# Turning a block of outputs back behind the next block's products in four steps of a fused attention and Fourier-mixing kernel, with four smaller changes of order and buffers

## The chip, the core and the metric

The kernel runs on one core of one Trainium2 chip. The metric is the device time of one execution in microseconds (us); lower is better. Three runs of the kernel before took 765.33, 768.76 and 773.62 us, so its median is 768.76 us. One execution was profiled; it took 765.44 us.

## What is computed

The first half is a decayed linear attention over 4 batches, 8 heads, 768 positions and 64 columns, in blocks of 64 positions with a running state:

```python
intra = np.einsum('bhic,bhjc->bhij', qb, kb) * Dmask[None]
intra = np.einsum('bhij,bhjd->bhid', intra, vb)
inter = np.einsum('bhid,bhde->bhie', qb * lam_pow[None], kv_state)
out[:, :, sl] = intra + inter
kv_state = lam_block[None, :, None, None] * kv_state + np.einsum('bhsd,bhse->bhde', kb_dec, vb)
```

Its output, laid out as x of shape 4 x 768 x 512, goes through a Fourier mix, a normalization and a two-layer network:

```python
mixed = np.real(np.fft.fft(np.fft.fft(x, axis=1), axis=2))
u = x + mixed
un = (u - mu) / np.sqrt(var + 1e-06)
ch = np.maximum(un @ w_ch1, 0.0) @ w_ch2
return u + ch
```

The weights come in as 64-bit floats and are converted on the chip to 32-bit ones.

## The kernel before, in words

The work lies in three stages.

**Attention** (the generator `attention`) goes through 12 steps, three per batch (SC = 3), each of 256 positions in two chunks of 128. Step i begins where the previous one has left scores in SBUF and the state's share of the output in PSUM, and then issues, in this order: `turn_k(i + 1)` and `turn_q(i + 1)`, which transpose the next keys and queries on TensorE and copy them to SBUF (L400, L401, L406, L407); `back(i - 1)`, which transposes the previous step's outputs `oT` back to rows (L476) and copies them out twice, once mirrored (L483 to L487, for one chunk L500 and L501); `to_state(i + 1)`, the products that add to the running state (L415) and VectorE's or ScalarE's reads of them (L425, L423); `within(i)`, the products of scores and values (L456) and the copies of the outputs to `oT` (L461); the loads of the values two steps on and the keys and queries three steps on; and `begin(i + 1)`: the next scores (L435), their reads with the decay mask (L441), GpSimd's scaling of the keys (L395) and decay of the state (L430), and the state's share of the next outputs (L450). `turn_q` also makes the queries times the powers of the decay, `qs`, on VectorE (L409); before, it reads the same PSUM tile as ScalarE's copy L407.

Each engine's order in this stage is the order in which the code is written (`strict`), interleaved by hand with the rest: after each of the three yields of a step, `PLAN` names units of other work. "w" is a third of a 512-column piece of weight conversion (L266, L267, L268, then L271, then L274 and L275: ScalarE does L267, VectorE the rest), "m" a unit of the Fourier mix of batch 0, "l" and "k" units of the first network layer. `REST` is the string of units behind the attention.

PSUM has eight banks, held by number here: pa_96 to pa_99 are banks 0 to 3 and go round for `psum_t` (transposes and scores); pa_100 and pm_101 are banks 4 and 5, the outputs being summed (`psum_o`); pm_102 and pm_103 are banks 6 and 7 and go round for `psum_a` and `psum_m`. Behind the attention `rest` is set so that all eight go round.

`oT` has one buffer: its copies (L461) wait until the previous outputs have been transposed (L476).

**Mix and first groups.** Then a scheduler orders the Fourier mix of batches 1 to 3, the normalization and the network for the first four groups of 256 rows (L735, L945, L952, L954, L960), beside the rest of the weight conversion. The first groups transpose their normalized rows in `turned_u` (L870, L871).

**Eight later groups in pairs.** The rest of the network runs as four pairs of groups with a seven-product scheme in two levels (L1230 for the first layer of pair 0, L1323 and L1397 otherwise, with VectorE's sums of the products, L1332 and L1405). `load_u(1)` loads the second pair's input into `ur` (L1093, two loads of 512 KB each). `ur` has one buffer, and the first pair's second layer uses it from SBUF as scratch for `sums_of_first`, four pieces at a time, written to memory through GpSimd's queue (L320, L322). Products' right-hand sums come from memory as `tx` (L1104, 256 KB each). L1140 is VectorE's first use of `ur`.

Of the kernel before, what the change touches and what calls it, by code (L numbers as in the profile page):

```python
# [17 lines left out]
ALU = mybir.AluOpType  # L18
# [59 lines left out]
def kernel(  # L78
# [69 lines left out]
    def P(i):  # L148
        return keep(i) if strict[0] else i
# [253 lines left out]
    def turn_q(i):  # L403
        for ch in range(2):
            pt = psum_t([128, HP, C])
            lead(P(nc.tensor.transpose(pt[:, hp, :], q_of[i % 2][:, ch, 128 * hp:128 * hp + 128], ident)) for hp in range(HP))  # L406
            P(nc.scalar.copy(qT[:, :, C * ch:C * ch + C], pt))  # L407
            if i % SC + ch:
                P(nc.vector.tensor_tensor(qs[:, :, C * ch:C * ch + C], pt, qpow, op=ALU.mult))  # L409

    def to_state(i):
        n, vt, kd = i % SC, v_of[i % 2], k_of[i % 2]
        chunks = (0, 1) if n < SC - 1 else (0,)
        pu = [(psum_t if unread[0] or i < 2 else psum_a)([128, HP, D]) for _ in chunks]
        lead(P(mm(pu[ch][HD[hi], hp, :], lhsT=kd[HD[ch], 2 * hp + hi, r, :], rhs=vt[HD[ch], 2 * hp + hi, r, :],  # L415
                start=(hp + r == 0), stop=(r == 1), skip_group_check=True))
             for hp in range(HP) for r in range(2) for ch in chunks for hi in range(2))
        with tc.high_priority(100):
            for ch in chunks:
                c = 2 * n + ch  # L420
                s_new = states[(c + 1) % 3]
                if c == 0:
                    P(nc.scalar.copy(s_new, pu[ch]))  # L423
                else:
                    P(nc.vector.tensor_tensor(s_new, s_new, pu[ch], op=ALU.add))  # L425
                if c < NC - 2 and ch == 0:
                    decayed(c + 1)
# [43 lines left out]
        if n == SC - 1:  # L471
            P(nc.vector.tensor_copy(z[:, :, 0:1], first))

    def turned(o, cols):
        px = psum_t([C, HP, 128])
        lead(P(nc.tensor.transpose(px[:, hp, :], o[:, hp, cols], ident)) for hp in range(HP))  # L476
        return px.rearrange("p h e -> p (h e)")

# [7 lines left out]
        P(nc.scalar.copy(x[0:n, 0:HM], px[0:n, 0:HM]))  # L486
        P(nc.scalar.copy(x[0:n, HM:DM], px[0:n, DM - 1:HM - 1:-1]))  # L487

    def back(i):
        b, n = divmod(i, SC)  # L490
        for ch in range(2):
            c = 2 * n + ch
            last = c == NC - 1
            cols = slice(C * ch, C * ch + C)
            if b in TURNED:
                if not last:
                    x = xn_[b, c] = new(xp, [C, DM], "x")
                    px = turned(oT[i], cols)
                    if n == 1 and ch == 0:
                        P(nc.vector.tensor_copy(x[:, 0:HM], px[:, 0:HM]))  # L500
                        P(nc.vector.tensor_copy(x[:, HM:DM], px[:, DM - 1:HM - 1:-1]))  # L501
                    else:
                        put(px, x)
                continue
            inside = b == INSIDE
            x = new(xn, [C, DM], "xn") if inside and c >= HC else new(xp, [C, DM], "x")
            if inside:
                xn_[b, c] = x
            put(turned(oT[i], cols), x, crossed=bool(ch))
            if c == 0:  # L510
                xd[b] = (dram.tile([S - 256, DM], F32, name=f"xa{b}"), dram.tile([257, DM], F32, name=f"xb{b}"),
                         dram.tile([C, DM], F32, name=f"xc{b}"))
                P(nc.sync.dma_start(xd[b][1][256:257], x[0:1]))
                if not inside:
                    P(nc.sync.dma_start(xd[b][2], x))
            elif not last:
                P(nc.sync.dma_start(xd[b][0][(c - 1) * C:c * C], x))
            if c >= NC - 2:
                P(nc.sync.dma_start(xd[b][1][(c - NC + 2) * C:(c - NC + 3) * C], x))
        if b not in TURNED or n == 0:  # L520
            return
        if n == 1:
            eo[b] = new_eo()
        work = [(2 * n - 1, oTs[i - 1]), (2 * n, oTs[i])]
        if n == SC - 1:
            work.append((2 * n + 1, oTs[i]))
        for m, o in work:
            px = turned(o, slice(C, 2 * C) if m % 2 == 0 else slice(0, C))
            if m < HC:
                put(px, eo[b][HC - 1 - m][1][:, 1, 0:DM][0:BLK[HC - 1 - m]], BLK[HC - 1 - m])  # L530
            else:
                u = xs[b, HC + NC - 1 - m] = new(xp, [128, DM], "x")
                put(px, u)
        if n == SC - 1:
            for t in range(HC):
                xs[b, t] = xn_.pop((b, t))

    def attention():

        n = B * SC  # L540

        def begin(i):
            first_ = from_state if i == n - 1 else scores
            first_(i)
            if i == 0:
                to_state(i)
            if i + 1 < n and i != n - 1:
                P(nc.gpsimd.tensor_copy(scored, sc[0][:, 0, 0, 0:1]))
                scale(i + 1)
            (scores if i == n - 1 else from_state)(i)  # L550
            if i % SC < SC - 1:
                decayed(2 * (i % SC) + 2)

        load_first()
        load(0, "qv")
        load(1, "kqv")
        scale(0)
        turn_k(0)
        sort(1)
        turn_q(0)  # L560
        load(2, "q")
        yield 0.1
        begin(0)
        load(2, "k")
        for i in range(n):
            if i:
                mirror(i - 1)
            yield 3.0
            if i + 1 < n:
                turn_k(i + 1)  # L570
                turn_q(i + 1)
            yield 2.0
            if i:
                back(i - 1)
            if i + 1 < n:
                to_state(i + 1)
            if i + 2 < n:
                sort(i + 2)
            within(i)
            if i + 2 < n:  # L580
                load(i + 2, "v")
            if i + 3 < n:
                load(i + 3, "kq")
            if i in TABLES:
                load_tables(TABLES[i])
            yield 4.0
            if i + 1 < n:
                begin(i + 1)
        back(n - 1)

    TABLES = {2: 1, 3: 2}


    LEADS = (0,)
# [786 lines left out]
    def deep_second(j, k):  # L1381
# [18 lines left out]
        def read(ps, s, m, first):  # L1400
            o = y[:, s, m * HM // 2:(m + 1) * HM // 2]
            if first and fresh:
                nc.scalar.copy(o, ps[:, 0:HM // 2])  # L1403
            else:
                V.tensor_tensor(o, ps[:, 0:HM // 2], o, op=ADD)  # L1405
            P.reads = P.reads + 1
            if P.sums and P.reads % 7 in (1, 3, 5):
                next(P.sums, None)

        if k == 0:  # L1410
            P.reads, P.sums = 0, None
# [24 lines left out]
        elif k == 3:  # L1436
            V.tensor_tensor(y22, y22, T, op=ADD)
            add_u(y21, y22, 1, 0)
            add_u(T, T, 0, 1)
            add_u(y22, y22, 1, 1)  # L1440
        elif k == 4:
            V.tensor_tensor(y22, y22, y12, op=ADD)
            V.tensor_tensor(y12, y12, T, op=ADD)
            if j < DEEP:
                run(P.sums)
                load_u(j + 1)
        elif k == 5:
            store(*who[1][1], yt[:, 1, 1])
            if j == PAIRS - 1:
                store(*who[1][0], yt[:, 1, 0])  # L1450
                for s in range(G):
                    store(*who[0][s], yt[:, 0, s], slice(0, HM))
        else:
            store(*who[0][1], yt[:, 0, 1], slice(HM if j == PAIRS - 1 else 0, DM))
            if j == PAIRS - 1:
                for m in (0, HM // 2):
                    store(*who[0][0], yt[:, 0, 0], slice(HM + m, HM + m + HM // 2))
            else:
                store(*who[1][0], yt[:, 1, 0])
                store(*who[0][0], yt[:, 0, 0])  # L1460
# [113 lines left out]
    def mixed(*parts):  # L1574

        parts = [[gen, t, 0.0] for gen, t in parts]
        while parts:
# [12 lines left out]
    t_half = 1.5 * t_mlp  # L1590
    lead_half = chain(half[0])

    PLAN = [("", "", "w"), ("", "w", "ww"), ("", "w", "ww"),
# [3 lines left out]
    REST = "mlmwwwllmmlmmlwlmmkwkwmkmwkwkmmwkwwkmmwkwwwwwwwwwwww"  # L1597
    first_two = {"w": w, "m": mix, "l": part(lead_half, 13.5), "k": part(half[0][1], 13.5)}

    def go(units):  # L1600
# [1 line left out]
            next(first_two[u], None)  # L1602

    next(att)
    for units in chain(PLAN):
        next(att)
        go(units)
    run(att)
    over[0] = True
    rest[:] = [0, 1, 2, 3, 4, 5, 6, 7]  # L1610
    go(REST)
    for u in "mlk":
        run(first_two[u])
# [53 lines left out]
```

## Time and profile before

| What | Value |
|---|---|
| time of three runs | 765.33, 768.76, 773.62 us |
| profiled execution: its own time | 765.44 us |
| span from first to last instruction | 763.7 us |
| around the span | 1.7 us |
| instructions in the span | 17114 |
| TensorE matmuls, weight loads | 6890, 6890 |
| ScalarE, GpSimd busy | 209.2 us, 202.5 us |
| instruction-queue packets (q8) | 54, together 0.88 MB |

Engines are PE (TensorE matmuls), PEld (its weight loads), DVE (VectorE), ACT (ScalarE), POOL (GpSimd) and SP (a queue that issues DMAs). A row of the view of instructions in order of time reads: start, duration, engine, line, operation, output<-inputs, count, and in brackets the idle time of the engine before it with what ended it. A row of the view of waits names who waited on which line for whom: total us, number, longest. "issue" is time in which an engine waited for nothing that the profile shows. Line numbers are those of the kernel before.

### The profile page before, as it was taken

The page shows a single profiled execution, that of the slowest core. Times are in us where ns is not written, and L with a number is a line of the kernel's source. Part 1 is how long each engine was busy: PE and PEld are TensorE (multiplying, and loading weights), DVE is VectorE, ACT ScalarE, POOL GpSimd, SP SyncE. Part 2 cuts the span into 40 slices and gives each one's busy share as a digit, 9 for nine tenths or more (in the row PEclk, how much of TensorE's full clock was granted, in tenths as well). Part 3 has the DMA queues.
Part 4 walks back from the last instruction along what each step waited for, and adds up shares of the span by engine and source line. Part 5 has one row for each costly group of instructions (what it writes and reads, how often), then busy time and mean ns, then how long its engine had stood idle before and what let it go on. Part 6 is the DMA issues. An engine that isn't in the chain of part 4 may idle for free.

```text
span 763.7 us, 17114 instructions
## 1 busy us (share of the span) xinstructions
PE 740.6 (97%) x6890; PEld 643.9 (84%) x6890; DVE 606.2 (79%) x1162; ACT 209.2 (27%) x487; POOL 202.5 (27%) x221
## 2 busy tenths in 40 slices
PE   7889999999999999999999999999999999999997
PEld 6788888884576586769648899999999999999997
DVE  5668967659999787587937999779986699748984
ACT  3354554553142111012002221034301341034310
POOL 3444433210042223300007922350024001320013
PEclk9999999999999999999999999999999999999999
DMA  9879986536353537522522476675645456456452
GB/s 202 247 179 228 241 247 187 176 103 190 97 168 130 127 115 207 142 93 56 124 56 97 152 221 215 220 247 180 189 125 181 142 163 190 131 170 187 140 139 69
DMA packets 132741, 123.50 MB, mean 162 GB/s; under 512 B 67007, under 2 KB 93247, under 8 KB 132663
## 3 DMA queue, kind: packets, MB, share of 16 engines
q1 hardware_dynamic: 126902, 103.66, 48.0%
q0 software_dynamic: 4032, 12.99, 5.0%
q10 hardware_dynamic: 1728, 5.77, 2.4%
q8 instruction: 54, 0.88, 0.5%
q14 instruction: 25, 0.20, 0.1%
HBM read 90.66 MB, written 31.73 MB: 160 GB/s over the span
## 4 chain that ended last, share of the span: by engine, by line
PE 47%; DVE 3%; DMA 2%; issue 1%; POOL 0%; SPq 0%; ACT 0%; DVEq 0%; POOLq 0%
PE p L1397 21%; PE p L1323 17%; PE p L1230 6%; PE pm L960 4%; DMA sd<-ur 1%; DMA ur<-utd 1%; DVE w1s L1036 1%; DMA tx<-td 0%; DVE un L792 0%; DVE e L807 0%; POOL rs L771 0%; DVE stt L766 0%; DVE hs L1245 0%; DVE hr L952 0%; DVE ha L1273 0%
## 5 line engine op out<-in xcount | busy, mean ns | idle before, releaser
L960 PE MATMUL pm<-w,hr 128*128 128x512 f32 x240 | 105.8, 594 | 0.1
L945 PE MATMUL pm<-ut,w 128*128 128x256 f32 x448 | 101.2, 380 | 1.1 <-ACT ut L871 0.7
L945 PEld LDWEIGHTS pm<-ut,w 128*128 128x128 f32 x448 | 84.0, 190 | 15.3 <-issue 3.3
L960 PEld LDWEIGHTS pm<-w,hr 128*128 128x128 f32 x240 | 44.9, 190 | 54.4 <-issue 50.9
L1418 POOL TENSOR_TENSOR y<-y,u 128x512 f32<-128x512 f32 x12 | 19.9, 1661 | 186.8 <-DVE y L1427 100.4
L1397 PE MATMUL p<-tx,sx 128*128 128x128 f32 x400 | 52.7, 275 | 0.0
L1397 PEld LDWEIGHTS p<-tx,sx 128*128 128x128 f32 x400 | 48.6, 192 | 0.0
L1332 DVE TENSOR_TENSOR ha<-p,ha 128x512 f32<-128x512 f32 x60 | 40.1, 685 | 8.3 <-PE p L1323 8.1
L1403 ACT COPY y<-p 128x128 f32<-128x128 f32 x48 | 12.8, 266 | 103.6 <-PE p L1397 103.1
L1405 DVE TENSOR_TENSOR y<-p,y 128x128 f32<-128x128 f32 x92 | 25.5, 284 | 16.1 <-PE p L1397 9.4
L954 ACT ACTIVATE hr<-pm 128x256 f32<-128x256 f32 x40 | 15.4, 385 | 81.9 <-PE pm L945 79.9
L1397 PE MATMUL p<-w,ha 128*128 128x128 f32 x288 | 37.4, 275 | 0.0
L1332 DVE TENSOR_TENSOR hs<-p,hs 128x512 f32<-128x512 f32 x39 | 26.2, 685 | 12.3 <-PE p L1323 12.3
L1397 PEld LDWEIGHTS p<-w,ha 128*128 128x128 f32 x288 | 34.9, 192 | 0.1
L267 ACT ACTIVATE e<-e,cvt 128x512 uint16<-128x512 uint16 x32 | 22.9, 721 | 40.4 <-DVE e L266 36.5
L1323 PE MATMUL p<-sx,tx 128*128 128x128 f32 x264 | 33.9, 275 | 0.0
L1323 PEld LDWEIGHTS p<-sx,tx 128*128 128x128 f32 x264 | 31.7, 192 | 0.0
L934 POOL DMA_INDIRECT out_dram<-y,ix x12 | 15.0, 1251 | 62.7 <-DVE y L997 50.7
L623 POOL DMA_INDIRECT fo<-xa,ix x6 | 15.4, 2566 | 59.1 <-DVE w L271 53.8
L1323 PE MATMUL p<-ur,w 128*128 128x128 f32 x216 | 28.0, 275 | 0.0
L435 PE MATMUL pa<-w 64*64 64x128 f32 x768 | 25.5, 271 | 2.3 <-issue 2.0
L1330 ACT COPY ha<-p 128x512 f32<-128x512 f32 x24 | 14.0, 584 | 49.2 <-PE p L1323 49.2
(342 smaller groups left out, 1932.2 us busy)
## 6 DMA issues: line engine op xcount, KB each, us to landing
tx<-td SPq DMA_DIRECT2D x84, 256.0 KB
tx<-sd SPq DMA_DIRECT2D x63, 256.0 KB
words<-in_moe_w_ch_dram SPq DMA_DIRECT2D x23, 512.0 KB
w<-in_v_dram SPq DMA_DIRECT2D x12, 512.0 KB
words<-in_k_dram SPq DMA_DIRECT2D x11, 512.0 KB
td<-tx SPq DMA_DIRECT2D x21, 256.0 KB
raw<-in_moe_w_ch_dram ACTq DMA_DIRECT2D x9, 512.0 KB
ud<-x SPq DMA_DIRECT2D x16, 256.0 KB
```

What stands on the lines that cost most here:

```text
L267: P(nc.scalar.activation(pw, pw, AF.Relu, bias=cvt[:, 0:1], scale=8.0))
L435: lead(P(mm(pss[r][hi][HD[ch], hp, :], lhsT=kT[HD[hi], r, hp, D * ch:D * ch + D], rhs=qT[HD[hi], hp, C * ch:C * ch + C], start=True, stop= ...
L623: P(gather(out=eo[b][a][1][0:n, 1, 0:DM], out_offset=None, in_=xa[:, :], in_offset=row_of(a, n)))
L945: P(nc.tensor.matmul(ps, lhsT=w1[:, c, 128 * fc:128 * fc + 128], rhs=ut[:, c, :], start=(c == 0), stop=(c == KO - 1)))
L954: P(nc.scalar.activation(t, ps, AF.Relu))
L960: return P(nc.tensor.matmul(ps, lhsT=hr[(fc - f0) // 4][:, fc % 4, 128 * i:128 * i + 128], rhs=w2[:, fc, :], start=(fc == f0), stop=(fc == ...
L1230: nc.tensor.matmul(ps, lhsT=s2.A[a][:, kt, 128 * i:128 * i + 128], rhs=U[b][:, kt, :], start=(first and kt == 0), stop=(kt == 1), skip_gro ...
L1323: nc.tensor.matmul(ps[:, 128 * i:128 * i + 128], lhsT=ab[m][0][:, 128 * i:128 * i + 128], rhs=ab[m][1], start=(start and i == 0), stop=Tru ...
L1332: V.tensor_tensor(o, p, o, op=ADD)
L1397: nc.tensor.matmul(ps[:, 0:HM // 2], lhsT=ab[m][0][i], rhs=ab[m][1][:, i, :], start=(start and i == 0), stop=(i == HF // 2 - 1), skip_grou ...
L1405: V.tensor_tensor(o, ps[:, 0:HM // 2], o, op=ADD)
L1418: nc.gpsimd.tensor_tensor(o, y, u, op=ADD)
```

## The change

Five edits:

1. `BEHIND = (1, 4, 5, 6)`: in these four steps `back(i - 1)` is issued after `within(i)` instead of before `to_state(i + 1)`, and its transposes use `psum_a` (banks 6 and 7); `to_state` uses `psum_t` there instead.
2. VectorE's scaled queries `qs` are made from ScalarE's copy `qT` in SBUF instead of from PSUM.
3. `PLAN`: one unit "w" is moved from behind step 2 to the second yield of step 3, and a unit "m" from there to step 4. `REST`: "wlmm" becomes "wmml" at one place.
4. `rest` and `turn["m"]`: ahead of the last units of the plan, and behind the attention, the banks go round in the order in which they were last used.
5. `load_u(1)` is called from the read that finds `sums_of_first` at its end, instead of after product 4 of the first pair's second layer.

```diff
             if i % SC + ch:
-                P(nc.vector.tensor_tensor(qs[:, :, C * ch:C * ch + C], pt, qpow, op=ALU.mult))
+                P(nc.vector.tensor_tensor(qs[:, :, C * ch:C * ch + C], qT[:, :, C * ch:C * ch + C], qpow, op=ALU.mult))
...
-        pu = [(psum_t if unread[0] or i < 2 else psum_a)([128, HP, D]) for _ in chunks]
+        pu = [(psum_t if unread[0] or i < 2 or i - 1 in BEHIND else psum_a)([128, HP, D]) for _ in chunks]
...
-    def turned(o, cols):
-        px = psum_t([C, HP, 128])
+    def turned(o, cols, psum=psum_t):
+        px = psum([C, HP, 128])
...
-            if i:
+            if i and i not in BEHIND:
                 back(i - 1)
             if i + 1 < n:
                 to_state(i + 1)
             if i + 2 < n:
                 sort(i + 2)
             within(i)
+            if i in BEHIND:
+                back(i - 1, psum_a)
             if i + 2 < n:
                 load(i + 2, "v")
...
+    BEHIND = (1, 4, 5, 6)
...
-            if P.sums and P.reads % 7 in (1, 3, 5):
-                next(P.sums, None)
+            if P.sums and P.reads % 7 in (1, 3, 5) and next(P.sums, P) is P:
+                P.sums = None
+                load_u(j + 1)
...
             if j < DEEP:
-                run(P.sums)
-                load_u(j + 1)
+                assert P.sums is None
...
-    PLAN = [("", "", "w"), ("", "w", "ww"), ("", "w", "ww"),
-            ("", "m", "mmm"), ("m", "mm", "mmm"), ("mm", "mmm", "mmmmm"),
+    PLAN = [("", "", "w"), ("", "w", "ww"), ("", "w", "w"),
+            ("", "w", "mmm"), ("m", "mm", "mmmm"), ("mm", "mmm", "mmmmm"),
...
-    REST = "mlmwwwllmmlmmlwlmmkwkwmkmwkwkmmwkwwkmmwkwwwwwwwwwwww"
+    REST = "mlmwwwllmmlmmlwmmlkwkwmkmwkwkmmwkwwkmmwkwwwwwwwwwwww"
...
-    for units in chain(PLAN):
+    for n, units in enumerate(chain(PLAN)):
         next(att)
+        if n == 3 * len(PLAN) - 1:
+            rest[:], turn["m"] = [6, 0, 1, 7], -1
         go(units)
     run(att)
     over[0] = True
-    rest[:] = [0, 1, 2, 3, 4, 5, 6, 7]
+    rest[:], turn["m"] = [7, 4, 5, 6, 2, 3, 0, 1], -1
     go(REST)
```

**VectorE in steps 2 and 3 of the attention.** Before (w is part of a weight tile, raw and e belong to the conversion, st is the state, fe and fo are the mix; L409 and L441 read PSUM banks):

```order
L271 SCALAR_TENSOR_TENSOR w_155<-raw_386,w_155 128x512
L274 SCALAR_TENSOR_TENSOR e_628<-raw_386,e_628 128x512
L275 SCALAR_TENSOR_TENSOR w_155<-w_155,e_628 128x512
L441 TENSOR_TENSOR w_155<-pa_98,decay 128x512
...
L409 TENSOR_TENSOR w_155<-pa_96,qpow 128x4x128
L409 TENSOR_TENSOR w_155<-pa_97,qpow 128x4x128
L609 TENSOR_TENSOR fe_646<-fo_647,x_639 128x512
L425 TENSOR_TENSOR st_149<-st_149,pm_102 128x256
```

The same place after the change, where L609 has become L612:

```order
L271 SCALAR_TENSOR_TENSOR w_155<-raw_386,w_155 128x512
L441 TENSOR_TENSOR w_155<-pa_97,decay 128x512
...
L409 TENSOR_TENSOR w_155<-w_155,qpow 128x4x128 x2
L274 SCALAR_TENSOR_TENSOR e_628<-raw_386,e_628 128x512
L275 SCALAR_TENSOR_TENSOR w_155<-w_155,e_628 128x512
L425 TENSOR_TENSOR st_149<-st_149,pm_103 128x256
L425 TENSOR_TENSOR st_150<-st_150,pm_102 128x256
L612 TENSOR_TENSOR fe_646<-fo_647,x_639 128x512
```

L274 and L275 have moved from ahead of step 2's reads of the scores to behind step 3's scaled queries, ahead of the reads of the state's products.

**TensorE behind the last step of the attention.** Before (un and e are normalized rows, ut their transposes, ys the mix between its two dimensions):

```order
L870 MATMUL pm_103<-ident,e_2210 128x128 x4
L747 MATMUL pa_100<-dt,ys_165 128x128
...
L945 MATMUL pa_97<-ut_2206,w_155 128x256 x4
L945 MATMUL pa_98<-ut_2206,w_155 128x256 x4
L870 MATMUL pa_99<-ident,un_2381 128x128 x4
L870 MATMUL pa_100<-ident,e_2384 128x128 x4
L945 MATMUL pm_101<-ut_2380,w_155 128x256 x4
```

After (L747, L870 and L945 have become L750, L873 and L948):

```order
L873 MATMUL pm_102<-ident,e_2210 128x128 x4
L750 MATMUL pm_103<-dt,ys_165 128x128
...
L948 MATMUL pa_97<-ut_2206,w_155 128x256 x4
L476 MATMUL pa_96<-ident,oT_2286 128x128 x4
L476 MATMUL pa_97<-ident,oT_2286 128x128 x4
...
L948 MATMUL pa_99<-ut_2206,w_155 128x256 x4
L873 MATMUL pa_96<-ident,un_2381 128x128 x4
L873 MATMUL pa_97<-ident,e_2384 128x128 x4
L948 MATMUL pm_103<-ut_2206,w_155 128x256 x4
L948 MATMUL pa_100<-ut_2380,w_155 128x256 x4
```

The banks differ throughout, and one group of four L945 with the old input now stands between the transposes and the first group that reads their result. The transposes L476 take the two banks that the two groups ahead of them have just filled.

**SP's queue ahead of the second pair.** Before:

```order
L1104 DMA tx_4599<-td_4253 128x512
L1093 DMA ur_4637<-utd_3250 128x1024
L1104 DMA tx_4598<-td_4252 128x512
L1093 DMA ur_4637<-utd_3326 128x1024
L1104 DMA tx_4600<-td_4254 128x512
```

After (L1093 and L1104 have become L1096 and L1107):

```order
L1107 DMA tx_4602<-td_4253 128x512
L1096 DMA ur_4581<-utd_3250 128x1024
L1096 DMA ur_4581<-utd_3326 128x1024
L1107 DMA tx_4601<-td_4252 128x512
L1107 DMA tx_4603<-td_4254 128x512
```

The second load of `ur` has moved ahead of one load of `tx`; the first stands where it stood.

More of the change, by code (lines that the diff above doesn't have):

```diff
@@ L487, in put, with back @@
         P(nc.scalar.copy(x[0:n, HM:DM], px[0:n, DM - 1:HM - 1:-1]))
-    def back(i):
+    def back(i, psum=psum_t):
         b, n = divmod(i, SC)
@@ L497, in back @@
                     x = xn_[b, c] = new(xp, [C, DM], "x")
-                    px = turned(oT[i], cols)
+                    px = turned(oT[i], cols, psum)
                     if n == 1 and ch == 0:
@@ L508, in back @@
                 xn_[b, c] = x
-            put(turned(oT[i], cols), x, crossed=bool(ch))
+            put(turned(oT[i], cols, psum), x, crossed=bool(ch))
             if c == 0:
```

## The prediction

> **What bounds the kernel now.** I read first the page's busy times, then the stretches, then who TensorE waits for.
>
> ```profile
> PE 740.6 (97%) x6890; PEld 643.9 (84%) x6890; DVE 606.2 (79%) x1162; ACT 209.2 (27%) x487; POOL 202.5 (27%) x221
> ```
>
> ```profile
> 0.00:170.00 170.00, 154.95 (x3038) 140.40 (x3039) 117.53 (x226) 80.92 (x190) 64.71 (x82) 1.00 0.76 203
> 170.00:240.00 70.00, 69.66 (x245) 43.05 (x243) 68.86 (x148) 21.83 (x45) 12.58 (x4) 1.00 0.49 152
> ```
>
> The columns are the stretch, its length, the busy time of PE, PEld, DVE, ACT and POOL, the granted clock and the DMA share. TensorE is the bound almost everywhere, at a clock of 1.00. The change removes no matmul, so it can only win from TensorE's idle time: 763.7 - 740.6 = 23.1 us in all, 15.05 of it in the first 170 us. What ended the idle time that this change can reach, or move:
>
> ```profile
> PE pa L435 <- issue: 2.0, 2, 1.4
> PE pa L450 <- issue: 1.4, 1, 1.4
> PE p L1397 <- DVE y L1405: 1.4, 1, 1.4
> PE pa L400 <- DVE w L441: 1.1, 1, 1.1
> PE pa L456 <- issue: 1.0, 1, 1.0
> PE pm L456 <- issue: 0.9, 1, 0.9
> PE pa L476 <- DVE w L409: 0.9, 2, 0.6
> PE pm L945 <- ACT ut L871: 0.7, 1, 0.7
> PE pm L870 <- ACT oT L461: 0.7, 1, 0.7
> ```
>
> The five waits for engines come to 1.4 + 1.1 + 0.9 + 0.7 + 0.7 = 4.8 us, 0.6% of the run. That is nearly all that edits of this kind can win; the four "issue" rows, 5.3 us, are a matter of their own (term D).
>
> **A. The weight unit and the queries (steps 2 and 3).** VectorE's order there, with two of TensorE's three stalls and the start of step 4:
>
> ```profile
> 44.69 1.15 DVE L271 SCALAR_TENSOR_TENSOR w<-raw,w 128x512 f32<-128x512 uint32 x1
> 45.77 0.68 DVE L274 SCALAR_TENSOR_TENSOR e<-raw,e 128x512 uint16<-128x512 uint16 x1
> 46.48 0.69 DVE L275 SCALAR_TENSOR_TENSOR w<-w,e 128x512 f32<-128x512 f32 x1
> 47.09 0.68 DVE L441 TENSOR_TENSOR w<-pa,decay 128x512 f32<-128x512 f32 x1
> 51.00 1.27 DVE L409 TENSOR_TENSOR w<-pa,qpow 128x512 f32<-128x512 f32 x2
> 55.34 0.42 DVE L425 TENSOR_TENSOR st<-st,pm 128x256 f32<-128x256 f32 x1 [0.73 <-POOL st L430]
> 55.68 1.15 DVE L611 TENSOR_TENSOR fo<-fo,x 128x512 f32<-128x512 f32 x1
> 57.42 0.68 DVE L441 TENSOR_TENSOR w<-pa,decay 128x512 f32<-128x512 f32 x1
> ```
>
> ```profile
> 47.92 1.16 PE L400 MATMUL pa<-ident,w 128*128 128x128 f32 x8 [1.10 <-DVE w L441]
> 51.73 1.25 PE L476 MATMUL pa<-ident,oTs 128*128 128x128 f32 x8 [0.58 <-DVE w L409]
> 58.64 1.09 PE L400 MATMUL pa<-ident,w 128*128 128x128 f32 x8
> ```
>
> The stall at 47.92 is a bank that waits for the first L441, which ended at 47.77, behind L274 and L275. With these two gone from there, L441 can start where L274 did, at 45.77, and free the bank at 46.45, so TensorE starts near 46.60: 1.3 us sooner. It would itself be ready at 47.92 - 1.10 - 0.3 = 46.5: the 0.3 is the shorter of the two waits on L409 (0.9 less 0.6), in step 2, which goes with edit 2 because the bank is free when ScalarE has copied it. The stall of 0.58 at 51.73 goes for the same reason, which makes 1.9 us at that place. L409 waits for ScalarE's copy of its chunk already, so edit 2 adds no wait for it.
>
> What is late next is step 3's L441. VectorE now has to do L274 and L275 (0.68 + 0.69) ahead of L425 instead of nothing, while one L615 moves behind. From 45.77, four L441 at 0.6 and the three copies that now fill the 1.5 us up to 51.00 end at 49.7, L409 twice at 51.0, the conversion at 52.3, the first L425, GpSimd's decay (the idle 0.73) and the second L425 at 53.9, L609 (as long as L409), L611 at 1.15 and L613 (as long as L425) at 55.9. The first L441 then ends at 56.6 and TensorE starts L400 at 56.7 or, since the four reads are paced 0.6 us apart, effectively at 57.1, against 58.64. So **1.5 us** stay. If nothing waits, 1.9 and some 0.1 of refilling per stall, 2.1; if L275 runs at L271's 1.15 or worse and L611 too, 0.8.
>
> **B. Banks by age behind the attention.**
>
> ```profile
> 138.29 0.63 PE L870 MATMUL pm<-ident,e 128*128 128x128 f32 x4 [0.67 <-ACT oT L461]
> 156.33 0.92 PE L945 MATMUL pm<-ut,w 128*128 128x256 f32 x3 [0.73 <-ACT ut L871]
> ```
>
> ```profile
> 137.73 0.41 DVE L832 TENSOR_TENSOR ds<-pm,bs 128x256 f32<-128x256 f32 x1
> ```
>
> ```profile
> 143.53 0.38 ACT L954 ACTIVATE hr<-pm 128x256 f32<-128x256 f32 x1 [1.34 <-PE pm L945]
> 152.57 1.08 ACT L864 ACTIVATE e<-x,sh,rs 128x256 f32<-128x256 f32 x2
> ```
>
> L870 waited 0.67 us for its bank, whose last read is L832 (ended 138.14; the row names ScalarE, which ended later). It now takes another; but the next products L747 take the bank that L832 reads, so they start where L870 started, four transposes (0.45) sooner: 0.45 won. The transposes L476 now take the two banks just filled: the last four wait for the second group's L954, which starts 0.2 us behind its group and takes 0.38, 0.58 in all, while the first four take 0.45: 0.2 lost with the signal. L870's last pair, now at 156.33 - 0.73 - 0.60 = 155.0, comes one group (0.38 + 1.34 = 1.72 from one L954 to the next) sooner, less than the 0.25 won so far: 153.0, and meets L864, which then ends at 152.57 + 1.08 - 0.25 = 153.4: 0.4 lost. The group put behind it covers L871, so the 0.73 (0.9 with refilling) is won. Sum 0.45 - 0.2 - 0.4 + 0.9 = **0.7 us**, between 0.2 (L864 later) and 1.4 (both stalls gone, nothing added).
>
> **C. The second pair's load.**
>
> ```profile
> 484.85 0.38 SPq L1104 DMA_DIRECT2D tx<-td  x1
> 485.29 0.42 SPq L1093 DMA_DIRECT2D ur<-utd  x1
> ```
>
> ```profile
> 477.98 6.31 DMA sd<-ur
> 485.29 5.15 DMA ur<-utd
> ```
>
> L1140 waits for the second `ur` load and holds up L1405, which frees TensorE's bank. That load moves ahead of one `tx`: 485.29 - 484.85 = 0.44 us sooner at issue, and 256 KB less ahead of it. In the 5.15 us the queue moves this load's 512 KB and what is ahead, at most 1 MB more, so 256 KB are up to 0.9 us. The first load does not move, since it waits for the last `sd<-ur` (landed 484.29), whatever the call's place in the program. TensorE's whole wait there is the 1.4 in the rows above. Gain 0.44 to 1.4; I take **0.8**. The overtaken `tx` is read two products later and comes some 1.5 us later; it is covered.
>
> **D. Turning back behind the outputs.** No wait in steps 1, 4, 5 and 6 is for an engine that `back` holds up. Eight transposes (58.64 to the next group 59.57, 0.9 us) swap places with products. Banks 6 and 7 are free and `oT`'s copies, which now wait for the transposes, still precede L450; the copies out go into ScalarE's idle time. That is worth nothing by itself. But the steps contain the "issue" stalls:
>
> ```profile
> q8 instruction: 54, 0.88, 0.5%
> ```
>
> ```profile
> 23.04:35.24 12.20, 10.73 (x254) 9.96 (x254) 10.34 (x18) 4.93 (x11) 5.82 (x6) 1.00 1.00 287
> 64.95:74.50 9.55, 8.68 (x253) 8.09 (x254) 7.37 (x15) 4.69 (x12) 3.70 (x4) 1.00 0.90 223
> 42.27:44.02 1.75, 1.75 (x64) 1.69 (x64) 1.00 0.05 16
> ```
>
> Stalls of this kind lie 254 matmuls apart, and TensorE's 13,780 instructions over 54 packets are 255 instructions, or 127 matmuls with their loads, to a packet. I read them as TensorE running ahead of its instruction queue where matmuls are short (the last row: 64 L456 in 1.75 us, 0.22 for eight) and DMA is busy. The borders stay at the same count of matmuls, so a swap of 0.9 us for 0.22 ahead of a border costs 0.65, and behind it wins 0.65. In step 1 one border each way, nothing; in steps 4 and 5 the border falls in L456, ahead of the moved transposes: 0.65 lost twice; in step 6 in L435, behind them: 0.65 won. Sum **-0.6 us**, from -1.9 (each a loss) to +1.3.
>
> The Trainium skill ("Runtime: NRT & Kernel Launch", Instruction fetch mechanics) says that fetching in blocks of 256 instructions is mostly hidden. By that rule D would be 0 and the gain 2.8 us; the issue rows above speak against it here.
>
> **E. The queries' new source.** L409 has two SBUF inputs now; its time stays (0.68 from PSUM, L441's, L274's 0.68 from SBUF) unless GpSimd works:
>
> ```profile
> 62.73 1.25 DVE L613 TENSOR_TENSOR fe<-fe 65x255 f32<-65x255 f32 x1
> 64.25 0.41 DVE L615 TENSOR_TENSOR fo<-fo 65x255 f32<-65x255 f32 x1
> ```
>
> ```profile
> 54.68 0.62 POOL L430 TENSOR_TENSOR st<-st,qpow 128x256 f32<-128x256 f32 x1 [3.62 <-DVE st L425]
> 62.31 1.40 POOL L389 COPY w<-words 128x1024 f32<-128x1024 f32 x1 [1.00 <-DMA words<-in_k_dram]
> ```
>
> L613 took three times its twin's time and ended 0.3 us after L389. L409 can meet L430 (0.62) in the eight steps whose state decays. VectorE mostly has idle time behind it, so I take **-0.2**, from 0 to 8 x 0.62 = -5.0. The Trainium skill ("SBUF — State Buffer", SBUF: two separate sides) states an exclusive lock between a VectorE instruction with two SBUF inputs and a GpSimd one that reads SBUF, held for the whole instruction. Taken at its full length this speaks against edit 2 and is rival 1 below; the two L613 and L615 rows agree with it.
>
> **Sum.** 1.5 + 0.7 + 0.8 - 0.6 - 0.2 = 2.2 us, so the profiled execution's 765.44 would become 763.2. TensorE stays the bound behind each place, and VectorE's full stretch from 170 on starts from a TensorE result, so the gain is carried on. That execution lies 3.3 us below the median of the runs; against 768.76 the same gain gives **766.5 us**.
>
> **The rivals.**
> 1. *VectorE's port decides; slower.* If L409 is held up by a whole L430 in eight steps and L441 with it, 5.0 us come instead of E's 0.2: 765.44 - 2.4 + 5.0 = 768.0, on the median's scale 771.4. It decides where VectorE has no idle time between L409 and L441; against it speak the idle 0.73 above and waits for products in most steps. 12%.
> 2. *The instruction stalls go.* If borders or latencies shift so that steps 4 to 6 stall no more, the rows' 1.0 + 0.9 and step 6's part of L435's 2.0 (0.6, the rest being the 1.4 of step 0) come back, 2.5 in place of -0.6: gain 2.2 + 0.6 + 2.5 = 5.3, 760.1, or 763.5. 13%.
> 3. *It does not do what it says.* The attention's gain is eaten by VectorE's full 170 to 240 us and by loads that set the pace, the second `ur` load lands as late as before: 0 to 0.5, so 768.5. The 98% VectorE share there speaks for it, the TensorE result ahead of it against. 20%.
>
> **How the numbers follow.** The forecast has 55%. Its terms' ranges, not all at one end, give a gain of -0.5 to 5, or 763.8 to 769.3; with rivals 1 and 2 and the runs' own spread of 8 us I give 761.5 to 771.5. One per cent, about what a measurement of this kernel can tell from no change, is 7.7 us, more than the 4.8 us of reachable waits. Faster by over 1% needs all of rival 2 and all of the bounds' upper ends: 6%. Slower by over 1% needs rival 1 with more than its price: 3%. Within 1%: 91%.
>
> **What would show it.** Right: no L400 wait on L441 near 46.5 and no L476 wait on L409; L400 of step 4 between 56.5 and 57.5; the first L945 with the new `ut` 0.5 to 1 us less far behind L456 of the last step; L1397's wait on L1405 between 0.2 and 0.9; stalls of about 1.6 in L456 in steps 4 and 5 and under 0.3 in step 6. Wrong: a wait on L441 over 1 us in step 3 or 4 (A), L409 over 1 us long beside L430 with a TensorE wait behind it (E), or issue stalls that do not lie at multiples of 127 matmuls (D).

## The result: slower, with the time lost in steps 3 to 6 of the attention

The changed kernel took 778.54 us (median of 4 runs, 777.74 to 779.56), the kernel before, timed beside it, 767.15 us (765.33 to 773.62). The ratio is 1.012, with a 95% interval from 1.008 to 1.017. The prediction said 766.5 us within 761.5 to 771.5 and gave a kernel slower by over 1% a chance of 3%: it was wrong in size and in sign.

The profiled execution of the changed kernel took 777.92 us, with a span of 776.1. Its page begins:

```profile
PE 746.0 (96%) x6890; PEld 646.8 (83%) x6890; DVE 608.1 (78%) x1162; ACT 209.0 (27%) x487; POOL 199.7 (26%) x221
```

The same 6890 matmuls now have 5.4 us more of busy time, and TensorE's idle time is 776.1 - 746.0 = 30.1 us where it was 23.1. That makes the 12.4 us of the span: 7.0 of idle time and 5.4 of slower work. The stretch from 50 to 110 us, first of the kernel before and then of the changed one (columns: stretch, length, busy PE, PEld, DVE, ACT, POOL, granted clock, DMA share, GB/s):

```profile
50.00:110.00 60.00, 56.58 (x1419) 52.16 (x1417) 46.85 (x85) 30.09 (x73) 23.78 (x24) 1.00 0.87 226
```

```profile
50.00:110.00 60.00, 47.21 (x1066) 42.29 (x1064) 40.47 (x72) 21.96 (x54) 19.21 (x20) 0.91 0.68 168
```

In the same 60 us TensorE starts 1066 matmuls instead of 1419, at a granted clock of 0.91 instead of 1.00. The DMA engines are less busy as well (a share of 0.68 instead of 0.87), so it is not more traffic that holds TensorE up. In this stretch the loads of the values land 4.3 us (median) after they leave, no later than in experiment 1 below (4.8), where TensorE hardly waits for them: they leave late. What TensorE waited for in the changed kernel:

```profile
PE pa L415 <- DMA w<-in_v_dram: 5.0, 2, 2.8
PE pa L456 <- issue: 3.7, 2, 2.9
PE pa L435 <- issue: 3.1, 2, 1.7
PE pm L456 <- issue: 2.9, 1, 2.9
PE pa L400 <- DVE w L441: 2.2, 2, 1.9
```

The values' load (`w<-in_v_dram`) heads the list. In the kernel before there was one wait for it, at 17.93 us:

```profile
PE pa L415 <- DMA w<-in_v_dram: 1.1, 1, 1.1
```

The waits that terms A, B and C were about, L476 on L409, L870 on `oT`, L945 on `ut` and L1397 on L1405, have gone, and A's wait of L400 on L441 has shrunk to 0.29 in step 3; the 1.9 in the row above is a new one, behind step 6. The long waits in order of time, from TensorE's timeline of the changed kernel:

```profile
55.70 0.32 PE L456 MATMUL pa<-sc,w 64*64 64x128 f32 x1 [2.93 <-issue]
...
74.93 1.16 PE L415 MATMUL pa<-w,words 64*64 64x64 f32 x64 [2.21 <-DMA w<-in_v_dram]
80.75 0.47 PE L456 MATMUL pm<-w,w 64*64 64x128 f32 x1 [2.92 <-issue]
91.24 1.99 PE L415 MATMUL pa<-w,words 64*64 64x64 f32 x64 [2.84 <-DMA w<-in_v_dram]
101.28 0.94 PE L400 MATMUL pa<-ident,w 128*128 128x128 f32 x6 [1.89 <-DVE w L441]
```

**Why the values are late** is seen on SP. SP issues its DMAs one after another, and one that waits holds up all behind it. First the kernel before, then the changed one, in the steps 4 and 5:

```profile
65.69 0.38 SPq L380 DMA_DIRECT2D w<-in_v_dram  x1
...
71.62 0.34 SPq L517 DMA_DIRECT2D xa<-x  x1
72.17 1.23 SPq L517 DMA_DIRECT2D xa<-xn  x1
75.13 0.38 SPq L380 DMA_DIRECT2D w<-in_v_dram  x1
```

```profile
70.14 0.35 SPq L517 DMA_DIRECT2D xa<-x  x1
70.59 0.38 SPq L380 DMA_DIRECT2D w<-in_v_dram  x1
71.07 0.65 SPq L380 DMA_DIRECT2D words<-in_k_dram  x1
...
85.08 0.34 SPq L517 DMA_DIRECT2D xa<-x  x1
85.63 0.34 SPq L517 DMA_DIRECT2D xa<-xn  x1
86.06 0.40 SPq L380 DMA_DIRECT2D w<-in_v_dram  x1
```

Before, the stores of `back(i-1)` (L517) leave some 3 us ahead of the values' load, which waits only for the products that read its buffer. Now the stores and the load leave together: the load stands behind the stores, and they wait for ScalarE. ScalarE in step 5 of the changed kernel:

```profile
83.43 0.59 ACT L461 COPY oT<-pa 128x512 f32<-128x512 f32 x1 [6.89 <-PE pm L476]
...
85.18 0.43 ACT L484 COPY xn<-pm 128x256 f32<-128x256 f32 x1
```

The outputs' copies (L461) start only when the moved transposes L476 are done, and the four copies of `back` come behind them. The second store waits for the last copy, which ends at 85.61, and leaves at 85.63. The load of the values follows at 86.06. The wait for values at 91.24 is the price: the load arrives just then.

### The profile page after: what moved, and what is told of

Read it like the earlier page. It is cut to its first block, busy times and chain, and to the rows that moved or that the text cites. A ratio compares the mean times of both kernels' runs of the same rounds, so it can differ in the third digit from the quotient of the medians.

```text
span 776.1 us, 17112 instructions
## 1 busy us (share of the span) xinstructions
PE 746.0 (96%) x6890; PEld 646.8 (83%) x6890; DVE 608.1 (78%) x1162; ACT 209.0 (27%) x487; POOL 199.7 (26%) x221
## 3 DMA queue, kind: packets, MB, share of 16 engines
HBM read 90.66 MB, written 31.73 MB: 158 GB/s over the span
## 4 chain that ended last, share of the span: by engine, by line
PE 49%; DVE 3%; issue 0%; POOL 0%; ACT 0%; DVEq 0%; POOLq 0%
PE p L1400 23%; PE p L1326 17%; PE p L1233 6%; PE pm L963 4%; DVE w1s L1039 1%; DVE un L795 0%; DVE e L810 0%; POOL rs L774 0%; DVE stt L769 0%; DVE hs L1248 0%; DVE hr L955 0%; DVE hs L1247 0%; DVE ha L1276 0%; DVE x L841 0%; DVE x L840 0%
## 5 line engine op out<-in xcount | busy, mean ns | idle before, releaser
L948 PE MATMUL pm<-ut,w 128*128 128x256 f32 x432 | 97.8, 379 | 0.3 <-DVE hr L955 0.3
L948 PEld LDWEIGHTS pm<-ut,w 128*128 128x128 f32 x432 | 81.1, 190 | 14.0 <-issue 3.4
L435 PE MATMUL pa<-w 64*64 64x128 f32 x768 | 26.9, 284 | 3.4 <-issue 3.1
L441 DVE TENSOR_TENSOR w<-pa,decay 128x512 f32<-128x512 f32 x24 | 16.4, 683 | 16.1 <-PE pa L435 16.1
L435 PEld LDWEIGHTS pa<-w 64*64 64x64 f32 x768 | 23.8, 141 | 5.7 <-issue 5.0
```

Source lines behind the costliest of these rows:

```text
L435: lead(P(mm(pss[r][hi][HD[ch], hp, :], lhsT=kT[HD[hi], r, hp, D * ch:D * ch + D], rhs=qT[HD[hi], hp, C * ch:C * ch + C], start=True, stop= ...
L441: P(nc.vector.tensor_tensor(sc[hi][:, r], pss[r][hi], decay[:, hi::2, 1 - r:1 - r + C], op=ALU.mult))
L948: P(nc.tensor.matmul(ps, lhsT=w1[:, c, 128 * fc:128 * fc + 128], rhs=ut[:, c, :], start=(c == 0), stop=(c == KO - 1)))
```

## The experiments

Each ratio is to the kernel before, timed beside it on the same chip, with its 95% interval. Where two experiments are compared, the ratios are compared, and 0.1% is 0.77 us.

### 1. No step moved

The change without its first step; the queries, the weight unit, the banks and the second pair's load stay changed.

```diff
-    BEHIND = (1, 4, 5, 6)
+    BEHIND = ()
```

> All of the change except the first step: `back` stands ahead of the products in every step again. Theory (SP's queue: the stores of `back`, which wait for copies out that now come after the transposes, stand ahead of the loads of values, keys and queries): the stores stand where they stood, loads leave within 1 us of the times of before (v loads near 56, 65, 75, 84 us), L415's waits on the values' DMA (2.2 and 2.8) go; the other three steps keep their gain of some 2 to 3 us, so 762 to 765. Rival 1 (instruction fetches alone: the 2.93 us stall in L456 at 55.7 comes before any store has moved): that stall stays, 2 to 3 us worse, 766 to 769. Rival 2 (the queries from SBUF or the weight unit a step later cost it): it stays near 777.

Measured: 766.78 us, ratio 0.9985 (0.9966 to 1.0005). So the first step of the change costs 1.0121 - 0.9985, that is 1.4% or 10.4 us; with the two intervals that is some 7 to 14 us. The time is in rival 1's range and not in the theory's 762 to 765: the other three steps didn't bring their 2 to 3 us. Its values' loads leave at 67.10, 77.13 and 85.94, and no wait of over 0.7 us on them is left. But the stall in L456 near 55 stays (2.76 at 55.36), as rival 1 said: that one doesn't come from the moved transposes. Experiments 7 and 8 are about it.

### 2. Step 1 alone

```diff
-    BEHIND = (1, 4, 5, 6)
+    BEHIND = (1,)
```

> The change with `back` behind the outputs in step 1 only, where it issues no store on SP (the first batch stays in SBUF). Theory (stores ahead of loads): as fast as with no step moved, within 1.5 us, 762 to 766. Rival (what costs is the transposes standing behind the products, and the banks they take): a quarter of the loss, some 3 us, stays, 766 to 769.

Measured: 767.49 us, ratio 0.9990 (0.9972 to 1.0007), no different from experiment 1, although in us it lies in the rival's range (766 to 769), as experiment 1 does. In step 1 the first batch's rows stay in SBUF and `back` stores nothing: transposes and copies behind the products are harmless there, without stores.

### 3. The loads ahead of `back`

All four steps moved as in the change, and only the order of the calls turned round, so that SP gets the loads first:

```diff
+            if i + 2 < n:
+                load(i + 2, "v")
+            if i + 3 < n:
+                load(i + 3, "kq")
             if i in BEHIND:
                 back(i - 1, psum_a)
-            if i + 2 < n:
-                load(i + 2, "v")
-            if i + 3 < n:
-                load(i + 3, "kq")
```

> The change with its four steps moved, but in them the loads of step i+2's values and of step i+3's keys and queries are issued ahead of `back`, so that no store stands ahead of them on SP's queue. Theory (stores ahead of loads): v loads leave near 56, 65, 74, 84 us again, L415's waits on the values go, 763 to 767. Rival 1 (instruction fetches in the steps with moved transposes): stalls of 2.9 us stay in L456 of steps 4 and 5, 769 to 774. Rival 2 (the transposes behind the products hold up the state's or scores' chain): 775 to 778, as with the whole change.

Measured: 769.79 us, ratio 1.0015 (0.9993 to 1.0038). Of the 10.4 us, 1.0121 - 1.0015 = 1.06%, 8.1 us (some 4 to 12 with the two intervals), are the order on SP alone. SP of this kernel, with the loads near the times of before (65.69, 75.13 and 83.87) and the stores behind them:

```profile
65.19 0.37 SPq L380 DMA_DIRECT2D w<-in_v_dram  x1
...
71.28 0.37 SPq L517 DMA_DIRECT2D xa<-x  x1
76.13 0.38 SPq L380 DMA_DIRECT2D w<-in_v_dram  x1
...
82.48 0.38 SPq L517 DMA_DIRECT2D xa<-xn  x1
86.30 0.38 SPq L380 DMA_DIRECT2D w<-in_v_dram  x1
```

L415 no longer waits for the values. Yet the kernel is 0.30% (2.3 us) behind experiment 1, about as much as the intervals can tell apart, so my theory may not have had all of it, and rival 1's range (769 to 774) held the time. Its stalls on instructions in L456 were 1.62 at 64.56 and 1.97 at 75.65. The next experiment tries another cause.

### 4. ScalarE's queue in step 6

In step 6 of the changed kernel ScalarE's and VectorE's timelines show a second queue that the move went past:

```profile
98.45 0.43 ACT L484 COPY xn<-pm 128x256 f32<-128x256 f32 x1
98.72 0.23 ACT L684 COPY fe<-fe 65x2 f32<-65x2 f32 x1
```

```profile
98.98 0.42 DVE L688 TENSOR_TENSOR fe<-fe 65x257 f32<-65x257 f32 x1 [3.28 <-ACT fe L684]
...
100.45 0.68 DVE L441 TENSOR_TENSOR w<-pa,decay 128x512 f32<-128x512 f32 x1
```

L684 is a copy of two columns for the folding of the first batch. VectorE stood 3.28 us for it with L441 queued behind, and L441 frees the bank that L400 wants: the 1.89 at 101.28. Without the move (experiment 1) the four copies of `back` are done long before, and L684 follows the outputs' copies at once:

```profile
85.89 0.59 ACT L461 COPY oT<-pm 128x512 f32<-128x512 f32 x1
86.37 0.20 ACT L684 COPY fe<-fe 65x2 f32<-65x2 f32 x1
```

So experiment 3 again, without step 6:

```diff
-    BEHIND = (1, 4, 5, 6)
+    BEHIND = (1, 4, 5)
```

> Loads ahead of `back` as before, and `back` behind the outputs in steps 1, 4 and 5 only, no longer in step 6, where four copies of `back` stood ahead of L684 on ScalarE and VectorE's L688 waited 1.35 us for it. Theory (ScalarE's queue is the second loss): L688's wait goes, L400's wait of 1.43 on L441 near 92 falls under 0.6, 767.5 to 769.3. Rival (what is left of the loss is instruction fetches in steps 4 and 5 alone): the time stays at 769.5 to 770.5 though the wait goes.

Measured: 767.91 us, ratio 0.9993 (0.9979 to 1.0007). VectorE no longer waits for L684, and L400's wait of 1.43 on L441 near 92 has gone. The step from 1.0015 is 0.22%, 1.7 us, but the two intervals overlap widely, so this size is not shown; what is shown is the queue and the wait. What is left to experiment 1, 0.08% or 0.6 us, is within the error. The profiled execution took as long as experiment 3's (770.36 and 770.40), so the gain is one of the medians alone. Its stalls on instructions in L456 were 0.16 at 66.17 and 2.08 at 77.40, so they moved without the time following.

### 5. The wait alone

The other direction: nothing moved (as in experiment 1), but in steps 4, 5 and 6 the loads stand on SP behind a 512-byte store that has to wait for the scaled scores. The store is the one thing added to what the kernel computes.

```diff
+            if i in HELD_UP:
+                mark = dram.tile([1, C], F32, name=f"mark{i}")
+                P(nc.sync.dma_start(mark, sc[0][0:1, 0, 0, :]))
+                loads(i)
...
-    BEHIND = (1, 4, 5, 6)
+    BEHIND = ()
+    HELD_UP = (4, 5, 6)
```

> The change without its first step (no transpose and no copy moved), but in steps 4, 5 and 6 the loads of values, keys and queries stand on SP behind a 512-byte store of the scaled scores, which is ready some 4 us behind the products, as long as the stores of `back` made them wait. Theory (the wait on SP's queue is the main loss): v loads leave 3 to 4.5 us behind the products' end, L415 waits on the values in two steps, 5 to 9 us slower than without the wait, 772 to 776. Rival (the moved transposes and ScalarE's later copies make the loss, the loads only go along): 766 to 769.

Measured: 773.14 us, ratio 1.0054 (1.0036 to 1.0072), 0.69% or 5.3 us above experiment 1. SP and, behind it, TensorE:

```profile
70.10 0.24 SPq L597 DMA_DIRECT2D mark<-w  x1
70.43 0.38 SPq L380 DMA_DIRECT2D w<-in_v_dram  x1
...
80.29 0.24 SPq L597 DMA_DIRECT2D mark<-w  x1
80.62 0.38 SPq L380 DMA_DIRECT2D w<-in_v_dram  x1
```

```profile
74.63 1.16 PE L415 MATMUL pm<-w,words 64*64 64x64 f32 x64 [1.18 <-DMA w<-in_v_dram]
...
84.83 1.16 PE L415 MATMUL pm<-w,words 64*64 64x64 f32 x64 [0.81 <-DMA w<-in_v_dram]
```

With not one transpose moved the same wait comes at the same place in two steps. It is shorter than in the change, where the transposes no longer stand ahead of L415 and cover 0.9 us of it. The rival falls: a small store in front of the loads is enough for about half of the loss (5.3 of 10.4 us, both with wide intervals). The waits for the values are only a part of it, though. Between the profiled executions of experiment 1 and of this one (767.02 and 774.08 us) TensorE's waits for the values grow by 1.9 us, its other idle time by 1.5 and its busy time by 3.6, most of the last at a clock of 0.66 behind two stalls on instructions, 2.64 us at 90.66 and 1.95 at 130.28. Experiment 1 has no such stall near 90, and its stall of 2.23 near 125 is followed by a clock of 1.00. Whether the late loads bring these stalls about isn't shown.

### 6. The first step alone

```diff
+    BEHIND = (1, 4, 5, 6)
...
-            if i:
+            if i and i not in BEHIND:
                 back(i - 1)
...
             within(i)
+            if i in BEHIND:
+                back(i - 1, psum_a)
```

> The kernel before with the first step of the change alone (`back` behind the outputs in steps 1, 4, 5 and 6). Theory: the whole loss is here, and the other steps' gain of 2 to 3 us is missing: 777 to 781, with L415 waiting 2 us or more on the values' DMA in two steps. Rival (the loss needs the earlier start of the other steps too, which uncovers the loads): 768 to 773.

> The kernel before with the first step alone, once more, for its profile. Theory: v loads leave near 71, 86 and 99 us in place of 66, 75 and 84; L415 waits 2 us or more on the values' DMA twice; L688 waits over 2 us on ScalarE's L684 in step 6 and TensorE's L400 behind it over 1 us; 780 to 785. Rival: without the early steps the stalls lie elsewhere, on instruction fetches above all.

Measured: 784.39 us (ratio 1.0202, 1.0161 to 1.0242) and 783.31 us (1.0212, 1.0174 to 1.0250). That is above the range of the first expectation and inside that of the second, and the second's profile has the same waits, those for the values longer:

```profile
PE pa L415 <- DMA w<-in_v_dram: 6.2, 2, 3.7
...
PE pa L400 <- DVE w L441: 3.0, 2, 1.9
```

Of the 3.0, 1.1 are the wait in step 2 that the kernel before has too. L688's wait for L684 is 4.3 us, where it was 3.28. The values' loads leave at 69.64, 84.13 and 99.29 us. The rival, that the early steps must uncover the loss, falls: without them it is larger. Why it is larger stays open.

### 7. The two early and the two late steps apart

The early ones (queries from SBUF and the weight unit):

```diff
-                P(nc.vector.tensor_tensor(qs[:, :, C * ch:C * ch + C], pt, qpow, op=ALU.mult))
+                P(nc.vector.tensor_tensor(qs[:, :, C * ch:C * ch + C], qT[:, :, C * ch:C * ch + C], qpow, op=ALU.mult))
...
-    PLAN = [("", "", "w"), ("", "w", "ww"), ("", "w", "ww"),
-            ("", "m", "mmm"), ("m", "mm", "mmm"), ("mm", "mmm", "mmmmm"),
+    PLAN = [("", "", "w"), ("", "w", "ww"), ("", "w", "w"),
+            ("", "w", "mmm"), ("m", "mm", "mmmm"), ("mm", "mmm", "mmmmm"),
```

> The kernel before with the two early steps alone: the queries scaled from SBUF and the weight unit a step later. Theory (term A wins its 1.5 to 2 us ahead of 52 us, and all of it and more is given back at the next instruction fetches: 2.8 us at 55, 2 us near 125, against 1.2 and 1.0 won back at 65 and 117): 767.5 to 769.5, ratio 1.000 to 1.002, with a wait of over 2 us on issue in L456 near 55. Rival (A's gain lasts): 766, ratio 0.998.

The late ones (banks by age with the swap of units in `REST`, and the second pair's load), which are the whole change with the lines above turned back and `BEHIND` empty:

```diff
-    BEHIND = (1, 4, 5, 6)
+    BEHIND = ()
```

> The kernel before with the two late steps of the change alone: PSUM banks by age behind the attention and the second pair's load sooner. Nothing ahead of 130 us moves. Theory (the prediction's terms B and C, 0.7 and 0.8 us): 1.5 us less than before, ratio 0.998. Rival (they are eaten downstream by VectorE's full stretch): ratio 1.000.

Measured: the late steps 766.07 us, ratio 0.9975 (0.9958 to 0.9993), as the theory said. The early steps 767.38 us, ratio 1.0001 (0.9983 to 1.0018): no gain. The ratio is the theory's, but its wait of over 2 us near 55 was 1.12.

### 8. The constants' load later

```diff
-    TABLES = {2: 1, 3: 2}
-    BEHIND = (1, 4, 5, 6)
+    TABLES = {4: 1, 5: 2}
+    BEHIND = ()
```

> The change without its first step, and the constants' loads (772 KB of cs, the indices, 323 KB of dt) issued two steps later, in steps 4 and 5. Theory (TensorE's instruction block is fetched behind the data that is already queued: with no store moved the fetch still started 7.6 us behind the border and the products stood for 2.76 us at 55.4): without 772 KB ahead of it the fetch starts 2 us or more sooner, that stall falls under 0.7, and the time by 2 us against the same kernel with early constants, 763 to 765.5. Rival (the border itself costs 2.8 us as soon as TensorE comes early, whatever is queued): the stall stays over 2, 766 to 768. Third (the constants only push another fetch back, in step 4 or 5): the stall moves there, 766 to 768.

Measured: 766.79 us, ratio 0.9981 (0.9963 to 0.9999), the time of experiment 1. The instruction packet that TensorE stood for did start sooner, at 50.96 where it was 52.83, but the stall only fell from 2.76 to 1.78. The theory wanted it under 0.7, with a time of 763 to 765.5. The time is that of the third possibility, and the stalls did move: in L456 of steps 4 and 5 they are 1.06 and 0.98, where experiment 1 had none and 0.57, and in L435 near 86 the stall grew from 0.72 to 2.08. The three kernels that bear on it, one row each, of experiment 8, of the early steps alone and of the late steps alone:

```profile
53.70 0.27 PE L456 MATMUL pa<-w,w 64*64 64x128 f32 x1 [1.78 <-issue]
```

```profile
53.59 0.27 PE L456 MATMUL pa<-w,w 64*64 64x128 f32 x1 [1.12 <-issue]
```

```profile
56.19 0.27 PE L456 MATMUL pa<-sc,w 64*64 64x128 f32 x1 [1.83 <-issue]
```

The last row matters most. Up to 130 us the late steps alone have the instructions of the kernel before in the same order, and that kernel's profile had no stall here at all. So a stall of this kind can differ by 1.8 us between two executions of the same order, and a single profile of it is no price.

## Why the prediction was wrong, step by step

**Term D failed, in the sentence "No wait in steps 1, 4, 5 and 6 is for an engine that `back` holds up", and in "the copies out go into ScalarE's idle time. That is worth nothing by itself."** The list of waits showed who was waited for, not who had slack. `back` is more than eight transposes and eight copies: from step 4 on it issues two or three stores on SP. I followed the transposes on TensorE and the copies on ScalarE and did not follow the stores on SP, where four loads stand behind them. The sum that I could have made, with step 4 of the changed kernel, whose moved transposes start when its products end and whose L406 is the last work ahead of step 5's L415:

```profile
66.75 1.09 PE L476 MATMUL pm<-ident,oT 128*128 128x128 f32 x8
...
71.49 1.23 PE L406 MATMUL pa<-ident,words 128*128 128x128 f32 x8
```

From the products' end to L415 are 72.72 - 66.8 = 5.9 us. The load needs 3.8 of them to leave (the transposes 1.1, the outputs' copies 1.1, the copies out 1.2, the rest the issue of the stores, 70.59 - 66.8 in all) and another 4.2 to land, at 74.79: 8.0 - 5.9 = 2.1 uncovered, and 2.21 were measured. Before, the load left at 65.69, with the products' end, and L415 didn't wait for it. The price in all, 8.1 us, is in experiment 3, and about half of the first step's loss comes with a store alone in experiment 5. The second queue, ScalarE's, holds L684, and with it L400 by 1.9 us in step 6; experiment 4 puts 1.7 us on it, within the error. ScalarE's idle time lay ahead of the products, and behind them there was a reader waiting.

**Term D's other half, the instruction stalls**, came out near its sizes in one execution where the loads are not disturbed: 1.6 in step 4, 2.0 in step 5 and 0.14 in step 6 of experiment 3, against 1.6, 1.6 and under 0.3. But experiment 4 had 0.2 and 2.1 in steps 4 and 5, in an execution of the same length. The borders do stay at the same count of matmuls, as forecast (step 3's at matmul 979 to 981, step 4's at 1232 to 1235, in every profile that stalls there); what comes sooner or later is the instruction packet. So the sum of -0.6 was no knowledge, and its agreement with experiment 3 may be luck: it took one execution's stalls for fixed. In the profile of before the waits on "issue" come to 6.5 us, in that of the late steps alone to 12.4; that execution was 2.5 us longer (767.98 and 765.44), though the median of its kernel is the lower one.

**A was right up to the next border and won nothing that could be measured.** In the changed kernel step 3's L400 started where the sum put it:

```profile
46.59 1.16 PE L400 MATMUL pa<-ident,w 128*128 128x128 f32 x8 [0.29 <-DVE w L441]
```

The forecast was "near 46.60", and the waits on L409 went. But step 4's L400 was to start between 56.5 and 57.5 and started at 57.89 with the early steps alone (58.64 before): the 1.12 us stall on instructions lies between. In the early steps alone the packet came at 50.95, and the first matmul behind it started at 53.59. TensorE, 1.5 us sooner than before, only waits there. That the whole of A is lost to such stalls fits the ratio of 1.0001 and the waits on "issue", which are 8.5 us there and 6.5 before, but is argued: the interval would still hold a gain of 1.3 us.

**B and C were right, as far as their sum shows it.** Their waits are gone, and together they measured 0.25% (1.9 us, interval 0.5 to 3.2) for 1.5 forecast. B's sign came true as well: the first group with the new `ut` starts 18.2 us behind the start of the last L456 in the changed kernel, where it was 19.0, and 0.5 to 1 less was forecast. C alone was not timed; its wait went wholly, where 0.2 to 0.9 was to stay.

**E was right in size, with the wrong partner.** One execution of the changed kernel has L409 at 1.63 and 1.52 us in two of twenty cases, where the longest was 0.69 before, and no engine waited for it. The two stood beside GpSimd's L395 and L389 and ended 0.5 us behind them; none of the long ones stood beside L430, whose price E and rival 1 were made of. So that E came out small is in part luck. Rival 1, VectorE's port at 5.0 us, fell. Rivals 2 and 3 fell with the forecast: none of them had the loads behind SP's stores in it.

## What to carry to other kernels

When a block is moved on one engine, write down every instruction that it issues on every other one, the DMA queue's own above all, and for each queue name what now stands behind the moved item and who reads it. A store that must wait for a copy should be issued behind the loads that wait for nothing else: here the order of stores and loads in these steps was worth some 8 us. And where profiles contain stalls that differ between executions of the same order, take them as a spread, not as a term.

## What the runs showed of the hardware that I had not expected

**Behind a long stall the clock is lower.** The 5.4 us of additional busy time are no more work: the matmuls are the same 6890. Windows of 5 us behind the four longest stalls of the changed kernel (the granted clock stands third from the end), and behind the 1.97 us stall of experiment 3:

```profile
55.70:60.70 5.00, 5.00 (x122) 5.00 (x125) 1.83 (x4) 1.07 (x2) 0.10 (x1) 0.66 0.24 66
74.93:79.93 5.00, 2.90 (x124) 2.65 (x124) 2.94 (x7) 0.37 (x1) 1.60 (x2) 1.00 0.83 156
80.75:85.75 5.00, 5.00 (x82) 4.34 (x84) 0.93 (x2) 2.18 (x6) 0.11 (x1) 0.66 0.01 3
91.24:96.24 5.00, 5.00 (x135) 4.83 (x136) 1.65 (x3) 0.00 (x0) 1.60 (x2) 0.69 0.66 116
```

```profile
75.65:80.65 5.00, 5.00 (x80) 4.50 (x82) 1.96 (x6) 2.18 (x6) 0.01 (x1) 0.66 0.55 143
```

The three slow windows lack 0.34, 0.34 and 0.31 of 5 us, together 5.0 us, which is nearly all of the 5.4. Of the stalls between 15 and 150 us in eleven profiles, one of each kernel, none under 1.85 us was followed by a lower clock; of the thirteen from 1.89 to 2.54 us six were, and of the ten of 2.64 us and more nine, at 0.50 to 0.69 over the next 5 us. So a long wait is often paid twice, and the loss of 12.4 us in the span is 7.0 of waiting and some 5 of a slow clock. The Trainium skill ("TensorE: Matmul & The Clock Gate", HAM oscillation) warns of idle gaps above some 3.4 us. Here the clock fell behind gaps of 2 us already.

**An instruction packet has a floor.** In the eleven profiles TensorE had 69 stalls on "issue" of over 0.6 us. Of these, 62 were on the first matmuls of a block of instructions, and every one ended 2.38 to 2.84 us after the block's packet had begun (median 2.60); the other seven were all on the same L415, at no border. The packet began about 1 us (median) behind the border before where the DMA engines were under 30% busy, and about 3 us (median, up to 8) where they were over 90% busy. The Trainium skill ("Runtime: NRT & Kernel Launch", Instruction fetch mechanics) calls this mostly hidden. By these figures it is hidden where 127 matmuls last longer than the two together, and here, where 64 L456 take 1.75 us and loads fill the DMA engines, it isn't.
